# x rows and kernel-gradient blocks moved in pieces of 4 KB and 1 KB instead of 256 and 64 bytes, in a fused state-space and gated feed-forward backward kernel

## The chip, the cores and the metric

The kernel runs on one core of a Trainium2 chip. The metric is the device time of one execution in microseconds (us), of which each kernel has several runs. Engines: PE is TensorE (with PEld, its weight loads), DVE is VectorE, ACT is ScalarE, POOL is GpSimd, SP is SyncE, which here does nothing but issue DMA transfers from one queue in order.

## The reference, cut to what matters

The kernel computes the output and all gradients of `x + A(norm(x)) + B(norm(x))`, where A is a long convolution whose kernel K comes from state-space parameters (L = 2048, D = 576, N = 128), and B a gated feed-forward block (F = 4608).

```
xn   = layernorm(x)
# A
K    = einsum("dn,dnl,dn->dl", Cc, exp(dt*A*l), dB).real
y    = irfft(rfft(pad(xn)) * rfft(pad(K)))[:L] + xn * Dskip
# B
gate = xn @ W_gate ; up = xn @ W_up
out  = x + y + ((gate * (gate > 0)) * up) @ W_down
```

Two gradients matter here. The weight gradients of W_gate and W_up are `xn^T @ dgate` and `xn^T @ dup`, with the 2048 rows of xn as the contracted axis. The gradient of K, called dk, is itself a convolution of xn and the output's gradient; the parameter gradients then sum over it.

## The kernel before

Both halves are written as generators whose steps are interleaved, and a scheduler then orders each engine's instructions. The feed-forward half works in 12 chunks of 384 columns of F. In each chunk it computes gate, up and their gradients (12 "units" of matmuls), and in the next chunk's time the weight gradients of the chunk before: four quarters of W_down's (`dw_down`, with rows of the output's gradient, `gq_dram`) and five pieces of W_gate's and W_up's (`dw_gu` and `dw_left`, with rows of xn, `xs_dram`). The row tiles come from HBM through three buffers, and are asked for two steps ahead:

```python
    def rows(self, c, i):                                   # c: chunk, i: step 0..8
        g, nc = self.g, self.g.nc
        for n in range(i, min(i + 3, 4 + NK)):
            if (c, n) not in self.R:
                t = self.dp.tile([P, ST, 144], BF16, name="rows")       # 3 buffers
                src = g.gq_dram[n] if n < 4 else g.xs_dram[n - 4]
                nc.sync.dma_start(t[:, :, 0:144 if n < 4 else min(P, D - (n - 4) * P)], src[:])
                self.R[(c, n)] = t
        return self.R[(c, i)]

    def dw_gu(self, c, k):
        # ... cut ...
        xs = self.rows(c, 4 + k)
        for src, dst in ((self.dgN, self.dWg), (self.duN, self.dWu)):
            ps = g.psum_mm.tile([P, 512], F32, name="ps_mm")
            for st in range(ST):
                nc.tensor.matmul(ps[:, :Fc], lhsT=xs[:, st, 0:P], rhs=src[:, st, :], start=(st == 0), stop=(st == ST - 1))
            ob = self.rp.tile([P, Fc], BF16, name="obw")                # 2 buffers
            g.bal.copy(ob[:], ps[:, :Fc], Fc)
            nc.sync.dma_start(dst[k * P:(k + 1) * P, f0:f0 + Fc], ob[:])
```

A gradient row tile fills its 144 columns; an x row tile fills 128 (or, the fifth, 64) of them, so each of its 16 rows per partition lands as a separate run of 256 (or 128) bytes.

The last stage of the pass `p1` makes dk, stores it to HBM row by row, and `p2` loads it back in blocks of 32 columns, which are runs of 64 bytes:

```python
    # dk_dram: [P, ST, DH]
            for n2 in range(ST):                           # end of p1
                S3 = self.dft(bp, self.s3_dram, n2)        # loads tile Sx for every second n2
                Ct = bp.tile([P, 1, 2, DH], BF16, name="bC1")
                nc.sync.dma_start(Ct[:], self.C[1][hf][:, n2])
                o = bp.tile([P, DH], BF16, name="dk_o")
                g.bal.copy(o[:], self.back2(S3, Ct, 0), DH)
                nc.sync.dma_start(self.dk_dram[hf][:, n2, :], o[:])
    # ... cut; in p2, 9 times for each half:
                nc.sync.dma_start(dkr[:], self.dk_dram[hf][:, :, dd0 - hf * DH:dd0 - hf * DH + SC])
```

`g.bal.copy` puts a copy on ACT or DVE, whichever has less to do by its account.

## Time and profile before

| | before |
|---|---|
| time, median of 6 runs | 2056.42 us (2043.02 to 2062.99) |
| span of the profiled run | 2053.0 us |
| PE busy / ACT busy / DVE busy | 90% / 72% / 71% |
| DMA packets / of them under 512 B | 390,368 / 196,042 |

From the page of the kernel before: span, engines, packets, the SP queue (q1), and the chain of work that ended last.

```profile
span 2053.0 us, 44388 instructions
PE 1850.4 (90%) x16776; PEld 1257.8 (61%) x16919; DVE 1464.2 (71%) x3633; ACT 1468.7 (72%) x3244; POOL 257.2 (13%) x321
...
DMA packets 390368, 372.86 MB, mean 182 GB/s; under 512 B 196042, under 2 KB 314058, under 8 KB 389898
...
q1 hardware_dynamic: 339402, 288.02, 47.1%
...
PE 40%; ACT 24%; DMA 16%; DVE 15%; issue 5%; SPq 1%; POOL 0%; ACTq 0%; DVEq 0%; POOLq 0%
```

PE is busy nearly all the time and half of all packets are small. DMA has 16% of the chain.

The view of the tile "rows" of the kernel before tells what ended PE's and PEld's idle time ahead of instructions that use it (us in total, times); gq are gradient rows, xs are x rows; "issue" is idle time in which the engine waited for nothing that the profile shows:

```profile
its engine sat idle before it (us, times) until:
  DMA rows<-gq_dram_97: 17.1, 6
  issue: 10.2, 40
  DMA rows<-xs_dram_92: 3.0, 2
  DMA rows<-xs_dram_91: 2.7, 3
  DMA rows<-xs_dram_89: 1.3, 2
```

In all 7.0 us of idle time, PE's and PEld's added up, ended with an x row load, out of 2053 (7.8 us in a second profile of the same kernel). The view of DMA issues says how long a transfer takes from issue to landing (times issued, KB, median us):

```profile
gT<-gT_dram SPq DMA_DIRECT2D x44, 640.0 KB, 5.9
xT<-xT_dram SPq DMA_DIRECT2D x44, 640.0 KB, 5.6
...
rows<-gq_dram_97 SPq DMA_DIRECT2D x12, 576.0 KB, 6.8
rows<-xs_dram_89 SPq DMA_DIRECT2D x12, 512.0 KB, 6.1
rows<-xs_dram_90 SPq DMA_DIRECT2D x12, 512.0 KB, 5.1
rows<-xs_dram_91 SPq DMA_DIRECT2D x12, 512.0 KB, 4.8
rows<-xs_dram_92 SPq DMA_DIRECT2D x12, 512.0 KB, 4.5
```

One step of `dw_gu` is 32 matmuls, which take 5.2 us in the chain (32 matmuls in 5.20 us), so two steps ahead is about 10 us ahead.

The trace also has a record of each DMA packet. For the SP queue, kernel before, by packet size:

```
bytes   packets   mean ns   sum over 16 engines, us
   64    36,864      11.1      411     dk loads
  128    26,625      13.0      346     the fifth x row tile (24,576 of them)
  256   109,700      18.4     2017     x rows (98,304 of them)
 2304    28,672     114.1     3271
 4608     8,704     225.4     1962     gradient rows
all queues, all sizes: 1453.6 us per DMA engine
```

From 64 and 256 bytes one gets, as an estimate, about 8.7 ns for a packet plus 0.038 ns a byte. The Trainium skill, "DMA: Bandwidth & Descriptors", section Specifications, gives 512 B as the least transfer for line rate. By the median packet the rate is 14 bytes/ns at 256 B, 19 at 512 B and 26 at 4608 B.

### The profile page before, as it was taken

How to read it: one execution, taken by the hardware profiler on the slowest of the kernel's cores; microseconds unless marked ns; L12 is line 12 of the kernel's file. 1: busy time of each engine (PE TensorE's matmuls, PEld its weight loads, DVE VectorE, ACT ScalarE, POOL GpSimd, SP SyncE). 2: the span in 40 equal slices, each digit the busy share in tenths (PEclk: the TensorE clock that was granted, in tenths of full speed). 3: DMA queues.
4: the chain of work that ended last, by engine and by line, in shares of the span. 5: the costliest groups of instructions: out<-in, count | busy, mean ns of one | idle time of the engine just before them, and what ended most of it. 6: DMA issues, size and time to landing. Idle time of an engine off the chain costs nothing.

```text
span 2053.0 us, 44388 instructions
## 1 busy us (share of the span) xinstructions
PE 1850.4 (90%) x16776; PEld 1257.8 (61%) x16919; DVE 1464.2 (71%) x3633; ACT 1468.7 (72%) x3244; POOL 257.2 (13%) x321
## 2 busy tenths in 40 slices
PE   5888897989999999998999999989899889888887
PEld 3664566556756766765766766666666565556555
DVE  7454771899988887896888778789777365654573
ACT  3664673899979879888879879868878645453562
POOL 6120010001101101101101102101101100110110
PEclk9999999999999999999999999999999999999989
DMA  9556889746755848747856755777755787987797
GB/s 331 208 174 171 264 210 225 195 138 130 184 143 125 192 135 183 151 135 183 185 142 123 176 151 113 172 202 186 169 132 121 198 220 214 255 193 173 214 249 201
DMA packets 390368, 372.86 MB, mean 182 GB/s; under 512 B 196042, under 2 KB 314058, under 8 KB 389898
## 3 DMA queue, kind: packets, MB, share of 16 engines
q1 hardware_dynamic: 339402, 288.02, 47.1%
q0 software_dynamic: 29248, 63.72, 20.1%
q10 hardware_dynamic: 21504, 18.29, 3.0%
q8 instruction: 132, 2.16, 0.4%
q14 instruction: 82, 0.67, 0.1%
HBM read 220.74 MB, written 149.20 MB: 180 GB/s over the span
## 4 chain that ended last, share of the span: by engine, by line
PE 40%; ACT 24%; DMA 16%; DVE 15%; issue 5%; SPq 1%; POOL 0%; ACTq 0%; DVEq 0%; POOLq 0%
PE ps_mm L248 10%; PE ps_mm L332 9%; PE ps_mm L290 7%; ACT osx L66 4%; PE ps_mm L319 2%; ACT YT L66 2%; PE pt L272 2%; ACT hN L66 1%; ACT ycs L813 1%; DMA rows<-gq_dram_97 1%; ACT ysn L811 1%; ACT ya L812 1%; ACT dgN L66 1%; ACT dhb L66 1%; ACT duN L66 1%
## 5 line engine op out<-in xcount | busy, mean ns | idle before, releaser
L66 ACT CAST osx<-ps_mm 128x288 bf16<-128x288 f32 x716 | 279.5, 442 | 54.7 <-PE ps_mm L290 53.4
L295 POOL DMA_DIRECT2D acc_dram<-osx x176 | 153.3, 871 | 1226.9 <-ACT osx L66 872.0
L290 PE MATMUL ps_mm<-wgT,dgT 128*128 128x288 bf16 x1152 | 218.8, 289 | 5.3 <-DVE upm L255 2.0
L290 PE MATMUL ps_mm<-wuT,duT 128*128 128x288 bf16 x1152 | 217.1, 290 | 0.0
L332 PEld LDWEIGHTS <-rows 128*128 128x128 bf16 x1536 | 148.1, 98 | 94.5 <-issue 5.5
L248 PE MATMUL ps_mm<-gT,wdT 128*128 128x512 bf16 x712 | 188.1, 385 | 0.4
L319 PE MATMUL ps_mm<-rows,hN 128*128 128x144 bf16 x2304 | 161.4, 229 | 17.7 <-DMA rows<-gq_dram_97 17.1
L255 DVE SCALAR_TENSOR_TENSOR upm<-rg,ps_mm 128x512 bf16<-128x512 bf16 x144 | 98.5, 684 | 106.6 <-PE ps_mm L248 74.2
L319 PEld LDWEIGHTS <-hN 128*128 128x128 bf16 x2304 | 152.3, 99 | 21.5 <-DMA rows<-gq_dram_97 10.0
L332 PE MATMUL ps_mm<-dgN,rows 128*128 128x384 bf16 x768 | 149.9, 331 | 2.9 <-DMA rows<-xs_dram_92 1.4
L332 PE MATMUL ps_mm<-duN,rows 128*128 128x384 bf16 x768 | 140.9, 326 | 0.0
L66 ACT CAST dhb<-ps_mm 128x512 bf16<-128x512 f32 x144 | 86.1, 598 | 74.6 <-PE ps_mm L248 72.8
L290 PEld LDWEIGHTS <-dgT 128*128 128x128 bf16 x1152 | 112.1, 99 | 38.3 <-issue 10.5
L290 PEld LDWEIGHTS <-duT 128*128 128x128 bf16 x1152 | 113.2, 99 | 30.4 <-issue 1.2
L290 PEld LDWEIGHTS <-hT 128*128 128x128 bf16 x1152 | 108.4, 99 | 36.4 <-issue 8.9
L248 PEld LDWEIGHTS <-wdT 128*128 128x128 bf16 x720 | 70.7, 99 | 79.6 <-issue 7.4
L813 ACT ACTIVATE ycs<-ya,hpcol 128x512 bf16<-128x512 f32 x144 | 110.1, 764 | 1.2 <-DVE Y L816 0.5
L253 ACT ACTIVATE rg<-ps_mm 128x512 bf16<-128x512 f32 x144 | 90.9, 631 | 27.5 <-PE ps_mm L248 24.6
L811 ACT ACTIVATE ysn<-yr 128x512 bf16<-128x512 f32 x144 | 96.1, 668 | 17.2 <-DVE yr L808 13.9
L812 ACT ACTIVATE ya<-yr 128x512 f32<-128x512 f32 x144 | 97.2, 675 | 15.6 <-DVE yr L808 15.4
L886 DVE TENSOR_REDUCE Sm<-pr 128x8 f32<-128x256 f32 x288 | 108.2, 412 | 0.0
L66 ACT CAST obw<-ps_mm 128x384 bf16<-128x384 f32 x105 | 50.0, 479 | 76.7 <-PE ps_mm L332 60.2
(3117 smaller groups left out, 4554.9 us busy)
## 6 DMA issues: line engine op xcount, KB each, us to landing
acc_dram<-osx POOLq DMA_DIRECT2D x192, 288.0 KB, 4.8
gT<-gT_dram SPq DMA_DIRECT2D x44, 640.0 KB, 5.9
xT<-xT_dram SPq DMA_DIRECT2D x44, 640.0 KB, 5.6
out_dram<-obw SPq DMA_DIRECT2D x96, 96.0 KB, 2.8
base_dram<-base SPq DMA_DIRECT2D x32, 288.0 KB, 4.0
f_base<-base_dram SPq DMA_DIRECT2D x16, 576.0 KB, 6.3
Sx<-s_dram SPq DMA_DIRECT2D x64, 128.0 KB, 3.6
rows<-gq_dram_94 SPq DMA_DIRECT2D x12, 576.0 KB, 4.5
```

The source lines that it names most:

```text
L66: self.nc.scalar.copy(out, in_)
L248: nc.tensor.matmul(ps[:], lhsT=w[:, k, fs], rhs=rhs[:, k, :], start=(k == 0), stop=(k == NK - 1))
L253: nc.scalar.activation(rg[:], ps_g[:], ACT.Relu)
L255: nc.vector.scalar_tensor_tensor(upm[:], rg[:], 0.0, ps_u[:], op0=ALU.is_gt, op1=ALU.mult)
L290: nc.tensor.matmul(ps[:, :DH], lhsT=lt[:, js], rhs=rh, start=(i == 0), stop=(i == len(mms) - 1))
L295: nc.gpsimd.dma_start(g.acc_dram[:, t, :, :], o[:], accum_op=ALU.add)
L319: nc.tensor.matmul(ps[:, (ft - f) * 144:(ft - f + 1) * 144], lhsT=self.hN[:, st, ft * P:(ft + 1) * P], rhs=gq[:, st, :], start=(st == 0), ...
L332: nc.tensor.matmul(ps[:, :Fc], lhsT=xs[:, st, 0:P], rhs=src[:, st, :], start=(st == 0), stop=(st == ST - 1))
L811: nc.scalar.activation(sn[:], yr[:], ACT.Sin, scale=-TWO_PI)
L812: nc.scalar.activation(ya[:], yr[:], ACT.Abs)
L813: nc.scalar.activation(cs[:], ya[:], ACT.Sin, scale=-TWO_PI, bias=g.hpcol[:])
L886: nc.vector.tensor_reduce(out=Sm[:, vi, s0 + dd:s0 + dd + DG, :], in_=pr[:], op=ALU.add, axis=AX.X)
```

## The change

The intent is to make both small-piece transfers contiguous on both sides. An x row tile is written densely at the front of its buffer, so that each partition gets one run of 4 KB (2 KB for the fifth). dk is collected on chip in one tile, already in the order of the blocks, stored once per half (9 KB a partition), and loaded in runs of 1 KB. Beside that, the S3 tiles get a pool of their own with two buffers in place of three.

```diff
-                nc.sync.dma_start(t[:, :, 0:144 if n < 4 else min(P, D - (n - 4) * P)], src[:])
-                self.R[(c, n)] = t
+                w = 144 if n < 4 else min(P, D - (n - 4) * P)
+                v = t[:].rearrange("p t d -> p (t d)")[:, 0:ST * w].rearrange("p (t d) -> p t d", d=w)
+                nc.sync.dma_start(v, src[:])
+                self.R[(c, n)] = v
...
-        self.dk_dram = two("dk_dram", [P, ST, DH])
+        self.dk_dram = two("dk_dram", [P, DH // SC, ST, SC])
...
             bp = self.pool(c, f"p1_c{hf}", 3)
+            dk = self.pool(c, f"p1_d{hf}", 1).tile([P, DH // SC, ST, SC], BF16, name="dk")
+            sp = self.pool(c, f"p1_e{hf}", 2)
             for n2 in range(ST):
-                S3 = self.dft(bp, self.s3_dram, n2)
+                S3 = self.dft(sp, self.s3_dram, n2)
...
-                o = bp.tile([P, DH], BF16, name="dk_o")
-                g.bal.copy(o[:], self.back2(S3, Ct, 0), DH)
-                nc.sync.dma_start(self.dk_dram[hf][:, n2, :], o[:])
+                g.bal.copy(dk[:, :, n2, :], self.back2(S3, Ct, 0).rearrange("p (g d) -> p g d", d=SC), DH)
                 yield 0.3
+            nc.sync.dma_start(self.dk_dram[hf][:], dk[:])
...
-                nc.sync.dma_start(dkr[:], self.dk_dram[hf][:, :, dd0 - hf * DH:dd0 - hf * DH + SC])
+                nc.sync.dma_start(dkr[:], self.dk_dram[hf][:, (dd0 - hf * DH) // SC])
```

## The prediction

> **What bounds the kernel.** The page has TensorE (PE) busy 1850 of 2053 us (90%), ScalarE and VectorE 72% and 71%, the DMA engines about 70% (47.1% by the SyncE queue). The chain that ended last is PE 40%, ACT 24%, DMA 16%, DVE 15%, issue 5%. PE's ordered stream bounds it: at most 200 us of PE idle time can be won, much of it in the first 100 us, the last 150 us and in waits on ScalarE copies.
>
> **What the change removes.** Of 390,368 packets about 164,000 are touched. By the trace's packet records a 256-byte packet takes 18.4 ns, a 128-byte one 13.0, a 64-byte one 11.1; 2304 bytes take a median 93 and 4608 bytes 178. The Trainium skill, "DMA: Bandwidth & Descriptors", Specifications, puts the size for line rate at 512 B and more; this trace agrees: 14 bytes/ns at 256 B, 26 at 4608 B. Summed over 16 engines, estimated:
> - Wide x rows: 98,304 packets of 256 B (1809 us) become 6,144 of 4 KB: 1106 us.
> - Narrow x rows: 24,576 of 128 B, 320 to 140 us.
> - dk loads: 36,864 of 64 B, 411 to 110 us.
> - dk stores: 32 transfers of 576-byte packets become 2 of 9 KB packets: 136 to 100 us.
>
> Saved: 1220 us, or 76 us per engine, 3.7 points of DMA share (70 to 66%). An x-row load needs 1.4 instead of 2.4 us of engine time, a dk load 0.4 instead of 1.4. Issues on the SyncE queue shorten from 0.53 to 0.32 us (60 x-row, 18 dk loads) and 30 of 0.32 us go: 26 us. The four gradient-row loads per chunk are already contiguous and don't change.
>
> **How much is on the critical path.** Little. x rows are fetched two steps (10 us of matmuls) ahead and land in 4.5 to 6.1 us; in the waits PE and its weight loads stand about 10 us in all for them. The long row wait (last quarter of the gradient rows, 17 us at matmuls, 10 us at weight loads) is for an unchanged transfer. To be won:
> 1. The last stage of the first kernel-gradient pass (311 to 351 us): PE idles 9 us of 40, DMA is 0.90 busy, and its stores stand in the in-order SyncE queue between loads that PE awaits. Without them: 3 to 6 us; the one 1.15 MB store lands 1 to 2 us later and gives some back.
> 2. Waits for x rows, the tail included (the chain has 5.2 us for such a load at 2030 us): 3 to 6 us.
> 3. Less queueing where DMA is 0.8 to 0.95 busy: 2 to 6 us.
>
> PE's instruction order, compared between the built programs, differs only in the first fifth, by a few us; later both halves interleave the same. Reshuffling should cost or bring under 5 us.
>
> **Prediction.** 2042 us, 0.7% faster; 80% range 2018 to 2059. Faster by over 2%: 0.09; within 2%: 0.88; slower: 0.03.
>
> **What would show it.** Packets fall to about 240,000, those under 512 B to about 36,000; the SyncE queue's share falls from 47.1 to 43%; PE busy time stays 1850 us; x-row loads land 0.5 to 1 us sooner, gradient-row loads as before; PE idle time shrinks by 10 us, chiefly at 311 to 351 us and at row loads.
>
> **What would make it wrong.** If DMA landing times fall generally, the 16% DMA share of the chain could give 20 to 40 us. If the strided copies into the dk tile are slower, the late store delays the first gradient sums and PE with them, or the reordered start costs PE, the gain vanishes.

## The result, and the profile after

| | before | after |
|---|---|---|
| time, median | 2054.14 us (2041.4 to 2062.99, 20 runs) | 2051.98 us (2046.47 to 2060.94, 10 runs) |
| ratio after / before | | 0.9997, 95% interval 0.9974 to 1.002 |
| span of the profiled run | 2053.0 us | 2044.4 us |
| DMA engine time, per engine | 1453.6 us | 1392.3 us |

A ratio here is the mean time of one kernel's runs over that of the other's in the same rounds, so it is not quite the ratio of the medians quoted. The predicted 2042 us against 2056.42 is a ratio of 0.993, which lies outside the interval: the change does not measurably alter the time. That the profiled run is 8.6 us shorter than that of before says nothing, as single runs of either kernel differ by more.

The page of the changed kernel, the same lines:

```profile
span 2044.4 us, 44327 instructions
PE 1846.3 (90%) x16776; PEld 1256.4 (61%) x16919; DVE 1464.1 (72%) x3633; ACT 1467.4 (72%) x3244; POOL 256.7 (13%) x321
...
DMA packets 236288, 372.86 MB, mean 182 GB/s; under 512 B 35818, under 2 KB 152042, under 8 KB 235562
...
q1 hardware_dynamic: 185322, 288.02, 44.0%
...
PE 39%; ACT 23%; DMA 16%; DVE 16%; issue 5%; SPq 1%; POOL 0%; ACTq 0%; DVEq 0%; POOLq 0%
```

Packets fell as predicted, and so did the SP queue's share. DMA's share of the chain is 16% as before.

What idle time ended with a row load in the changed kernel (the dots stand for waits that did not end with one):

```profile
its engine sat idle before it (us, times) until:
...
  DVE f_base L995: 8.0, 1
  DMA rows<-gq_dram_97: 5.3, 3
  DMA rows<-xs_dram_89: 4.8, 2
...
  DMA rows<-xs_dram_91: 0.3, 1
```

The x row waits are 5.1 us here and 1.1 us in the second profile of the changed kernel, so they did shrink, from 7.0 and 7.8. The wait for the gradient rows is split up otherwise: with the weight loads' part, which this view leaves out (10.0 us before, 11.3 after), it is 27.1 us before and 16.6 after, and one wait of 8.0 us that ended with DVE has come in.

And the landing times in the changed kernel:

```profile
gT<-gT_dram SPq DMA_DIRECT2D x44, 640.0 KB, 6.0
xT<-xT_dram SPq DMA_DIRECT2D x44, 640.0 KB, 5.6
...
rows<-gq_dram_97 SPq DMA_DIRECT2D x12, 576.0 KB, 6.2
rows<-xs_dram_89 SPq DMA_DIRECT2D x12, 512.0 KB, 6.0
rows<-xs_dram_90 SPq DMA_DIRECT2D x12, 512.0 KB, 4.7
rows<-xs_dram_91 SPq DMA_DIRECT2D x12, 512.0 KB, 5.2
rows<-xs_dram_92 SPq DMA_DIRECT2D x12, 512.0 KB, 3.8
```

Each of the x row lines is the median of only 6 to 11 landings, as the trace does not give every one, and they scatter. Over all five x row tiles together, worked out from the landing records, the mean is 4.9 us before (43 landings) and 4.4 us after (45), and 5.0 and 4.4 us in the second profiles: sooner by about the 0.5 to 1 us that was forecast. xT and gT, which queue beside them, moved by 0.1 us at most.

The dk hand-over at the end of the first pass, from the SP timeline (start us, us, queue, line, transfer), kernel before. The row of line 682 is the last two small stores; the row of line 765 is the first dk load, which must wait for all of dk:

```profile
350.00 1.37 SPq L682 DMA_DIRECT2D dk_dram_150<-dk_o  x2
...
356.16 0.53 SPq L765 DMA_DIRECT2D dkr<-dk_dram_150  x1
```

The same in the changed kernel, with the single store:

```profile
347.17 0.45 SPq L686 DMA_DIRECT2D dk_dram_150<-dk  x1
...
354.62 0.50 SPq L768 DMA_DIRECT2D dkr<-dk_dram_150  x1
```

The stage itself ended 4 us sooner (last copy into dk at 346.6 us, before 350.6), but from its store to the first load 7.5 us pass in place of about 5, and the first POOL copy of the loaded block starts at 359.9 us against 360.1. So in this one pair of traces the gain in the stage was handed back at its end. In the second pair the longer hand-over is there again (7.5 us against 4.9), but the stage ended later in the changed kernel (357.3 us against 352.6), so that the change made it end sooner is not shown. Whether any of this matters to the time is what the experiments ask.

### The profile page after: what moved, and what is told of

The parts are those of the page before. It is cut to its first block, busy times and chain, and to the rows that moved or that the text cites. A ratio compares the mean times of both kernels' runs of the same rounds, so it can differ in the third digit from the quotient of the medians. Undisturbed runs are those within 1.5% of the kernel's fastest.

```text
span 2044.4 us, 44327 instructions
## 1 busy us (share of the span) xinstructions
PE 1846.3 (90%) x16776; PEld 1256.4 (61%) x16919; DVE 1464.1 (72%) x3633; ACT 1467.4 (72%) x3244; POOL 256.7 (13%) x321
## 2 busy tenths in 40 slices
DMA packets 236288, 372.86 MB, mean 182 GB/s; under 512 B 35818, under 2 KB 152042, under 8 KB 235562
## 4 chain that ended last, share of the span: by engine, by line
PE 39%; ACT 23%; DMA 16%; DVE 16%; issue 5%; SPq 1%; POOL 0%; ACTq 0%; DVEq 0%; POOLq 0%
PE ps_mm L248 9%; PE ps_mm L334 9%; PE ps_mm L290 6%; ACT osx L66 4%; PE ps_mm L321 2%; ACT YT L66 2%; PE pt L272 2%; DMA xt<-xg_dram 2%; DMA out_dram<-g_ob 2%; ACT hN L66 1%; ACT ysn L814 1%; ACT dgN L66 1%; ACT duN L66 1%; ACT ycs L816 1%; DMA acc_dram<-osx 1%
## 5 line engine op out<-in xcount | busy, mean ns | idle before, releaser
L321 PEld LDWEIGHTS <-hN 128*128 128x128 bf16 x2304 | 152.1, 99 | 17.8 <-DMA rows<-gq_dram_97 11.3
L290 PEld LDWEIGHTS <-hT 128*128 128x128 bf16 x1152 | 107.4, 98 | 37.5 <-issue 10.5
```

The lines of the kernel that those rows point to most:

```text
L290: nc.tensor.matmul(ps[:, :DH], lhsT=lt[:, js], rhs=rh, start=(i == 0), stop=(i == len(mms) - 1))
L321: nc.tensor.matmul(ps[:, (ft - f) * 144:(ft - f + 1) * 144], lhsT=self.hN[:, st, ft * P:(ft + 1) * P], rhs=gq[:, st, :], start=(st == 0), ...
```

## The experiments

Three theories went in. **O** (off the path): the transfers that became cheaper were not waited for. **C** (cancel): the x rows bring a gain and the dk part loses as much. **Q** (queue): all transfers would land sooner in emptier engines; that was item 3 of the prediction.

Several sections count in *units*: unit n is the start of the n-th ReLU of the feed-forward loop in the trace (144 in all, 12 per chunk, counted from 0), a mark which all versions share.

### The two parts alone, and no x rows at all

`rows_only` is the kernel before with only the four lines of `rows` changed; `dk_only` is the changed kernel with the `rows` of before. `no_x_rows` gives a wrong result:

```diff
+        if i >= 4:
+            return self.R[(c, 3)]          # the last gradient row tile in place of x rows
-        for n in range(i, min(i + 3, 4 + NK)):
+        for n in range(i, min(i + 3, 4)):
```

Expected of `rows_only`:

> Only the x-row loads write contiguous 4 KB (or 2 KB) runs; the dk part is as before. Theory O (off the path: x rows land well before PE needs them, so their saved engine time is not waited for): within 4 us of before. Theory C (cancel: rows gain, dk part loses as much): 6 to 12 us faster than before. Theory Q (queue: all transfers land sooner when the engines are less full): 8 to 15 us faster. In the profile DMA packets near 275,000 in all cases.

Expected of `dk_only`:

> Only the dk part (one tile, one late store, contiguous dk loads, two S3 buffers in place of three); x rows in 256-byte pieces as before. Theory O: within 4 us of before; the last dk copy comes about 4 us sooner but the first dk load is issued no more than 2 us sooner, since the one store takes 6 to 7 us where the last small one took 3. Theory C: 6 to 12 us slower than before. Theory Q: 2 to 5 us faster.

Expected of `no_x_rows`:

> Wrong result on purpose: the changed kernel with no x-row loads at all (the weight-gradient matmuls for gate and up use the last gradient-row tile instead). An upper bound for what any better x-row load can bring. Engine time falls by a further 85 us or so per engine. Theory O: 0 to 6 us faster than before. Theory C: 8 to 15 us faster. Theory Q: 15 to 25 us faster, and other loads (gT, xT) land at least 0.3 us sooner in the median.

| run | median | ratio to before | 95% interval | DMA engine time |
|---|---|---|---|---|
| rows_only | 2044.81 us | 1.0012 | 0.9983 to 1.0042 | 1380.2 us |
| dk_only | 2041.45 us | 0.9985 | 0.9957 to 1.0013 | 1419.5 us |
| no_x_rows (wrong result) | 2045.7 us | 1.0013 | 0.9986 to 1.004 | 1274.7 us |

(Before, in the same rounds: 2040.85 us.) Neither part gains or loses, so theory C falls. With no x row loads at all, 179 us less engine time than the kernel before, the time is the same. The wait of PE for x rows was then zero, and PE's idle time (span less busy) was 2049.9 - 1850.3 = 199.6 us, where the kernel before had 202.6. The 7 us of waits were not lost time that could be had here: PE stood idle as long without them. gT and xT landed at 6.0 and 5.4 us (before 5.9 and 5.6), so Q's sign, 0.3 us sooner in both, did not come either.

Where this could have been seen without any run, for nearly half of the program: the waits in the stretch from 500 to 1450 us of the kernel before. This is the only line there in which anything waits for a row load (engine, line, what for: us in total, times, longest):

```profile
PE ps_mm L319 <- DMA rows<-gq_dram_97: 2.4, 2, 1.4
```

Nothing waits there for an x row or for the buffer of an output store. And the engines' busy time in that stretch, of before (the columns are named in its first line; PEclk is the share of the TensorE clock that was granted):

```profile
core 0: us, PE busy (x) PEld busy (x) DVE busy (x) ACT busy (x) POOL busy (x), PEclk, DMA share, GB/s
500.00:1450.00 950.00, 897.46 (x8912) 626.84 (x8981) 788.71 (x1865) 801.54 (x1731) 117.85 (x122) 1.00 0.67 159
```

and of `no_x_rows`:

```profile
500.00:1450.00 950.00, 900.35 (x8907) 628.61 (x8979) 787.83 (x1863) 799.12 (x1732) 117.55 (x122) 0.99 0.57 145
```

PE is 94 to 95% busy there whether the DMA share is 0.67 or 0.57.

### A second profile of each kernel

`before_again` and `after_again` are the two kernels unaltered, one look each.

> The kernel before once more, for a second profile. If the differences of the two kernels' profiles at the same unit of the main loop (up to 8 us by 220 us, none by 450 us) come from the program, this profile lies within 1 us of the first one of before at each unit; if they are spread between runs, it differs by several us, chiefly before 450 us and after 1450 us.

> The changed kernel once more, for a second profile; same reading. I expect the 7 us lead at unit 14 (207 against 200 us) to be in the program's order and to come back, and what follows after unit 28 to differ between runs.

Time from unit to unit, in us:

| run | start to unit 32 | 32 to 104 | 104 to 140 | 140 to end | span |
|---|---|---|---|---|---|
| before | 493.1 | 950.4 | 514.4 | 95.0 | 2053.0 |
| before_again | 494.5 | 946.7 | 512.9 | 91.8 | 2045.8 |
| after | 490.0 | 947.5 | 512.1 | 94.8 | 2044.4 |
| after_again | 498.8 | 947.9 | 508.8 | 90.9 | 2046.5 |
| rows_only | 498.8 | 949.4 | 509.2 | 94.0 | 2051.3 |
| dk_only | 494.3 | 945.8 | 509.9 | 96.6 | 2046.5 |
| no_x_rows | 491.1 | 950.9 | 514.3 | 93.6 | 2049.9 |

The second profile of before is within 2 us of the first up to unit 32, but ends 7 us sooner; the two of after are 9 us apart at unit 32. The 7 us lead that after had at unit 14 (199.8 against 207.1 us) was not in its program, as I had expected: the second profile has that unit at 206.2 us. What the two kernels' profiles differ by is spread between runs. The middle column, 72 units or half of the loop, holds within 0.6% in all seven.

### The dk hand-over: no wait, and a shorter last store

`dk_free` (wrong result) lets the dk loads read a tensor that is ready early; `dk_split` sends half of dk at half of the stage.

```diff
# dk_free
-                nc.sync.dma_start(dkr[:], self.dk_dram[hf][:, (dd0 - hf * DH) // SC])
+                nc.sync.dma_start(dkr[:].rearrange("p t d -> p (t d)"), g.xT_dram[0][:, 0, :])
# dk_split
+                if n2 % 8 == 7:
+                    nc.sync.dma_start(self.dk_dram[hf][:, :, n2 - 7:n2 + 1, :], dk[:, :, n2 - 7:n2 + 1, :])
                 yield 0.3
-            nc.sync.dma_start(self.dk_dram[hf][:], dk[:])
```

> Wrong result on purpose: the changed kernel with its dk loads reading an early tensor of the same shape, so the kernel-gradient sums wait neither for the late store nor for the pass before it. An upper bound for item 1 of the prediction. If the dk hand-over is on the critical path: 5 us faster than before or more, gained between 300 and 450 us. If it is not (theory O for dk as well): within 4 us of before. Theory C (the late store eats the gain) needs at least 6 us faster.

> The changed kernel with the dk store in two halves, the first sent when half of the stage is done, so that the last store is 0.6 MB. Correct result. First dk load issued 2 to 4 us sooner than in the changed kernel after the last dk copy. Theory C: 3 to 6 us faster than the changed kernel. Theory O: within 4 us of before.

`dk_free`: 2052.5 us, ratio to before 1.001 (0.9982 to 1.0037). `dk_split`: 2052.41 us, 1.0011 (0.998 to 1.0042). In `dk_split` the second store was issued at 358.1 us and the first dk load at 362.7 us, 4.6 us later, where the changed kernel took 7.5 us in both of its profiles. That is the shortening expected, but other runs with the undivided store took from 5.3 us (`prep_first`, below) to 8.6 us (`dk_only`), so that the split brought it is not shown. In any case it did not show in the time, and neither did taking the whole wait away. So the first item of the prediction had nothing measurable behind it: the sums that wait for dk do not decide when the kernel ends.

### Added DMA time, badly aimed twice

If DMA time is off the path, adding some should cost little. `spare128` copies each x row tensor once more, DRAM to DRAM in 128-byte pieces, to a buffer nobody reads. `ballast` stores an on-chip weight tile in 64-byte pieces where each x row tile is first used.

```diff
# spare128, in rows()
+                if n >= 4:
+                    nc.sync.dma_start(g.spare[n - 4][:, :, :, 0:64], src[:].rearrange("p t (b d) -> p t b d", d=64))
# ballast, in dw_gu() and dw_left(), after self.rows(...)
+        nc.sync.dma_start(g.spare[k][:, :, 0:32], self.wgT[:].rearrange("p t d -> p (t d)").rearrange("p (b e) -> p b e", e=32))
```

> The changed kernel with a useless extra copy beside each x-row load, DRAM to DRAM in 128-byte pieces, to a buffer nobody reads: roughly 200,000 small packets, about 150 to 200 us more time per DMA engine, three times what the change saved, and 60 more issues on the SyncE queue. Theory O: 0 to 10 us slower than before. Theory Q: 20 us slower or more, and gT and xT land at least 0.5 us later in the median. Theory C says nothing beyond O here.

> The changed kernel with a useless store of an on-chip weight tile (64-byte pieces, 6,912 packets each) issued where each x row tile is first used, 60 in all, so the extra DMA time lies beside the x-row loads in every chunk and not piled up early: estimated 250 to 300 us more time per DMA engine, four times what the change saved. Theory O: under 12 us slower than before, and between unit 32 and unit 104 of the main loop the pace of the loop is the same as before within 3 us. Theory Q: 25 us slower or more, spread evenly over all chunks.

| run | median | ratio to before | DMA engine time | start to unit 32 | 32 to 104 | 104 to 140 |
|---|---|---|---|---|---|---|
| spare128 | 2166.25 us | 1.0601 (1.057 to 1.0631) | 1617.5 us | 610.8 us | 945.6 us | 507.1 us |
| ballast | 2173.22 us | 1.0601 (1.0572 to 1.063) | 1711.4 us | 522.5 us | 1008.3 us | 544.1 us |

Both missed what O expected by far, and both for a reason of their own. The spare copies depend on nothing but the x rows in HBM, so the scheduler moved them to the front: all were done by 650 us, the DMA engines were 0.94 busy from 100 to 490 us, and the whole loss of 118 us came before unit 32; the loop after unit 32 ran at its usual 945.6 us. `ballast` was spread as meant, and cost 58 us between units 32 and 104. Its waits from 500 to 1450 us say what it hit, an output store (two `obw` buffers) whose buffer ACT needs again:

```profile
ACT obw L66 <- DMA out_dram<-obw: 62.0, 18, 7.1
```

ACT stood 62.0 us there, about as much as the loop lost, and nothing waited for an x row. The store stands behind the ballast in the SP queue. The Trainium skill, "DMA: Bandwidth & Descriptors", section Queues, rings and completion order, says that on each DMA engine descriptors of one queue are consumed in ring order; these runs fit that. So extra DMA time can cost, where it stands ahead of something that is waited for. One thing else differs in these two runs and in `x_64B` below: the granted clock of the profiled run is lower (0.951, 0.957 and 0.961, before 0.975). In `spare128` PE was busy 1869.9 us in place of 1850.4 with as many matmul records, 19.5 of the 118 us. Whether the clock fell because PE stood idle more is not shown. That left the question which kind of curve the two kernels lie on.

### The piece size itself: 128 and 64 bytes

These two runs worsen just what the change improved. They are the changed kernel with the x rows read in smaller pieces from a padded view of an early tensor of the same kind (wrong result; same bytes, same number of transfers).

```diff
-                nc.sync.dma_start(v, src[:])
+                if n < 4:
+                    nc.sync.dma_start(v, src[:])
+                else:                       # e = 64 for x_128B, 32 for x_64B
+                    src = g.xT_dram[0].rearrange("p k t -> p (k t)").rearrange("p (b e) -> p b e", e=e*5//4)[:, 0:ST * w // e, 0:e]
+                    nc.sync.dma_start(t[:].rearrange("p t d -> p (t d)")[:, 0:ST * w].rearrange("p (b e) -> p b e", e=e), src)
```

> Wrong result on purpose (the x-row loads read an early tensor of the same size, so that nothing but the piece size differs): the changed kernel with x rows in 128-byte pieces, half of what they were before the change. By 13.0 ns a packet, 256 packets per engine and load, 3.3 us of engine time a load (before: 2.4, after: 1.6 measured). Slack theory (x rows are asked for two steps, some 10 us, ahead, and an output store has one 5 us step before its buffer is needed again; any load within that costs nothing): within 4 us of before. Rival (cost in proportion to DMA time, from the 122 us that the stores of the ballast run cost for 319 us of engine time): 15 to 25 us slower than before.

> As x_128B, with 64-byte pieces: 512 packets of 11.1 ns per engine and load, 5.7 us of engine time each, about 190 us more per engine in all than the changed kernel. Slack theory: 5.7 us exceeds one step of the loop (5.3 us), so output stores behind the loads start to hold their buffers: 15 to 90 us slower, with ScalarE waiting for output stores. Rival (in proportion): 60 to 75 us slower, spread over all waits.

The whole curve, with the engine time of one wide x row load (its packets per engine times their mean duration in that run):

| x rows in pieces of | one load, engine time | total per engine | ratio to before | units 32 to 104 |
|---|---|---|---|---|
| (no loads) | 0 | 1274.7 us | 1.0013 (0.9986 to 1.004) | 950.9 us |
| 4 KB (after) | 8 x 206 ns = 1.6 us | 1392.3 us | 0.9997 (0.9974 to 1.002) | 947.5 us |
| 256 B (before) | 128 x 18.4 ns = 2.4 us | 1453.6 us | 1 | 950.4 us |
| 128 B | 256 x 16.7 ns = 4.3 us | 1539.1 us | 1.0087 (1.0052 to 1.0123) | 951.1 us |
| 64 B | 512 x 15.6 ns = 8.0 us | 1744.3 us | 1.0488 (1.0449 to 1.0526) | 986.7 us |

This is a curve with a flat part and a rise. The straight line of the rival fits neither end: from the 100 us that `x_64B` costs for 291 us of engine time above before, removing all x row loads (179 us less) ought to bring some 60 us, and it brought nothing. My slack theory put the bend a little too far out: it wanted `x_128B` free, and it cost 18 us (the rival's number was right there); and `x_64B` cost more than the 90 us I allowed. The packets were also slower than estimated, 16.7 and 15.6 ns in the mean in place of 13.0 and 11.1, so the loads were longer than planned; their medians stayed at 13 and 11 ns, and the means rose through a slow part of them. The points differ in one more thing: before, the small pieces lie on the chip's side of the transfer, in `x_128B` and `x_64B` on HBM's side, so this is a curve of engine time and not of piece size alone.

The waits show in part how the rise comes about. In `x_128B`, PE's matmuls waited 3.0 us for x rows before 500 us and 3.7 us after 1900 us, PEld likewise 3.9 and 4.3 us, and never between. They do not account for the 18 us, and the profiled run of `x_128B` (2060.1 us) is only 7.1 us longer than that of before, so where the 18 us lie stays open. In `x_64B` the loop pays too, from 500 to 1450 us, and for the output stores, as in `ballast`:

```profile
ACT obw L66 <- DMA out_dram<-obw: 26.0, 8, 5.0
```

Even with 64-byte pieces, nothing in that stretch waits for an x row; what pays is the store queued behind it. The landing records of the transfers issued in that stretch bear it out. These stores landed in 2.9 us in the mean before, in 2.1 without x rows, in 3.7 in `x_64B` and in 4.7 in `ballast`. The stores of the POOL queue (`acc_dram`), which use the same DMA engines, took 5.1, 4.9, 5.0 and 5.0 us. So what slowed down stood behind the small pieces in their queue; fuller engines alone did not do it.

### The one long row wait

The longest wait for a row tile is for the last quarter of the gradient rows, 17.1 us at matmuls and 10.0 us at weight loads before. `prep_mid` and `prep_first` give PE the next chunk's weight transposes to do ahead of it:

```diff
                 for q in range(4):
                     self.dw_down(c - 1, q)
                     yield self.DN_US
-                self.prep_dn(c)
-                self.prep_gu(c)
+                    if q == 1:                # prep_mid: prep_gu stays behind the loop
+                        self.prep_dn(c)
+                    # prep_first: if q == 0: prep_dn(c), prep_gu(c)
```

> The changed kernel with the next chunk's transposes of the down weights placed between the second and third quarter of the down-weight gradients, to give PE work while the last quarter's gradient rows load, the longest row wait (17 us at matmuls and 10 us at weight loads before). If that wait is on PE's critical path: 8 to 20 us faster than before. If it is given back as other waits: within 4 us.

> The changed kernel with all of the next chunk's weight transposes right after the first quarter of the down-weight gradients, so that the last quarter's gradient rows have 5 us more. If prep_mid's 0.2% was real and due to that wait: 3 to 8 us faster than before and waits of PE for that tile under 8 us at matmuls and weight loads together. If not: within 4 us.

`prep_mid`: 2047.58 us, ratio 0.9978 (0.9955 to 1.0001). `prep_first`: 2047.33 us, ratio 0.9972 (0.9938 to 1.0005), in other rounds. The waits for gradient rows, matmuls and weight loads together, were 17.9 and 17.0 us. Both runs are edits of the changed kernel, and without the edit it waited 16.6 us in its first profile and 19.1 in its second (before: 27.1 and 22.7). So the edits did not shorten the wait, let alone to below 8 us, and these runs do not test what it costs. Both lean to a quarter of a per cent, and neither interval leaves out no effect; what the lean comes from, if it is real, is not known.

## Why the prediction was right or wrong

**The costs were about right.** Packets (236,288, predicted 240,000), packets under 512 B (35,818, predicted 36,000), the SP queue's share (44.0%, predicted 43%) and PE's work came as predicted. The x row loads landed about 0.6 us sooner, as predicted. The engine time saved was 61.3 us an engine (1453.6 - 1392.3), not 76: the 4 KB packets took 206 ns in place of 180, which is 10 us of the difference, and other transfers' times moved a little. (The prediction had set medians of large packets, 178 ns at 4608 bytes, beside means of small ones; the mean at 4608 bytes was 225.4.) "Within 2%" had been given 0.88, and the time is within the range.

**The size of the gain was wrong: 14 us forecast, 0.03% measured with 0.2% of uncertainty.** The step that failed is "How much is on the critical path", in all three of its terms: it counted waits that end with a transfer, and queueing that gets shorter, as time that the kernel would gain.

- *Item 1*, "3 to 6 us" from the last stage of the first kernel-gradient pass. PE's idle time from 311 to 351 us did not shrink (8.8 us before, 9.4 after). The stage ended 4 us sooner in one pair of traces and 4.7 us later in the other; the longer hand-over behind the late store, which the prediction feared, is in both. But taking the whole dk wait away brought nothing measurable (1.001), so the late store is not what ate the gain.
- *Item 2*, "waits for x rows, 3 to 6 us". The waits shrank about as forecast (7.0 and 7.8 us in the two profiles of before, where the prediction had read about 10, and 5.1 and 1.1 us in those of after), and the run without x rows has none, yet neither is faster. PE's idle time was to shrink by 10 us; it was 202.6 and 193.3 us in the two profiles of before, 198.1 and 200.5 in those of after, and 199.6 without any x row loads. The waits that went away came back as other idle time, so they were not time to be won.
- *Item 3*, "less queueing where DMA is 0.8 to 0.95 busy". The landing times of unchanged transfers did not fall in general: gT took 5.9 us before, 6.0 after and 6.0 without x row loads, xT 5.6, 5.6 and 5.4. Some did fall (the last quarter of the gradient rows from 6.8 to 6.2 us after the change, the output stores from 2.8 to 1.6 without x row loads), and even that brought no time.

"Reshuffling should cost or bring under 5 us" is not contradicted: both parts alone and the whole lie within their intervals of no change.

What replaced the explanation: both kernels lie on the flat part of a curve. x rows are asked for about 10 us before they are needed, land in about 5, and hold up the output stores behind them by less than those stores have to spare. The rise begins somewhere between the engine times of 256 and of 128 bytes. That the slack is the reason for the flat part is argued from the waits, which show no x row wait in the middle stretch; the flatness and the rise themselves are measured. What stays open: what the 5% of the loop in which PE stands idle are due to (ACT, DVE or PE's own order), and where the 18 us of `x_128B` lie, since its profiled run is only 7.1 us longer and two profiles of one kernel differ by more (9 us at unit 32).

## What to carry to other kernels

Before counting saved DMA time as a gain, look at the waits of one long stage, not of the whole program: here no engine waited there for the x rows or for what queues behind them, and 154,080 fewer packets brought nothing measurable. Take the suspect transfer away altogether in one wrong-result run; within its noise it bounds what any faster form of that transfer can bring. And when you add load to test for slack, see that it is issued where you mean it and know what stands behind it in the same queue.

## What the Trainium skill lacked or had wrong

- "DMA: Bandwidth & Descriptors", Why small descriptors are slow: it counts bus cycles and metadata bytes per packet but gives no time by size; a packet time of about 10.5 ns, for a 4 KB transfer of 64 packets issued from GpSimd, stands in the page's section Bandwidth. Here a packet took 11.1 ns at 64 B, 13.0 ns at 128 B and 18.4 ns at 256 B in the kernel before, about 8.7 ns plus 0.038 ns a byte by the first and the last; in padded reads of small pieces the mean was higher (15.6 ns at 64 B, 16.7 ns at 128 B).
- "Perfetto Trace Analysis", DMA Optimizations: it calls larger DMAs the primary optimization when HBM utilization is high but the kernel is DMA-bound, and the page's section Optimization Strategy says to find what blocks the gaps of the engine in question. Neither says that such a gap can go without any time being won: here x row waits went from 7.0 and 7.8 us to 5.1 and 1.1, DMA engines were 0.67 busy in the main stretch, and 154,080 fewer packets (390,368 - 236,288) changed the time by a ratio of 0.9997.
- No page that we found says that long transfers cost through stores queued behind them: 62.0 us of ACT waiting for output buffers in `ballast`, 26.0 us in `x_64B`, both between 500 and 1450 us, with no wait for the long transfer itself.
